# Chunk-selected attention with a top-1 expert layer: loads two pairs ahead, zero fill in four parts, sums folded earlier, bounds and row scalars in PSUM

## The chip, the cores and the metric

The kernel runs on one core of a Trainium2 chip. The metric is the device time of one launch in microseconds (us). Five engines work side by side, each taking its own instructions strictly in order: TensorE (PE, matmuls and transposes), VectorE (DVE), ScalarE (ACT), GpSimd (POOL) and SyncE (SP, which here only issues DMAs). They meet only through semaphores.

## The reference

Attention over 4 batches, 8 heads, 768 rows and 64 columns, in which each query keeps 6 of its causal chunks of 32 keys; then a top-1 mixture of experts with 8 experts, at most 80 tokens in each.

```python
ub = np.sum(np.maximum(q * k_min, q * k_max), axis=-1)     # bound of a chunk, 24 chunks
top_chunks = np.argsort(np.where(causal, ub, -1e9), axis=-1)[..., -6:]
scores = np.where(sel & (pos_q >= pos_k), q @ k.T / 8, -1e9)
attn = softmax(scores) @ v                                  # [4, 8, 768, 64]
x = attn.transpose(0, 2, 1, 3).reshape(3072, 512)
probs = softmax(x @ w_gate); e = argmax; keep the 80 highest gates of each expert
out[tok] = gate * (relu(x[tok] @ w1[e]) @ w2[e])            # all other rows are zero
```

## The kernel before, in words

Work goes by **pairs**: 16 pairs of heads (4 batches, 4 pairs each), one pair in one round of the main loop. For a pair the q, k and v of two heads lie side by side, 128 columns wide. In round i the program issues, in this order:

- `scores(i)`: six steps. In a step PE multiplies keys by queries into one of two PSUM tiles `SC` (L476), adds -65536 where a chunk was not selected (L482), and ACT takes the exponential into `EXB`, piece E0 to E5 (L487). POOL then zeroes the part above the diagonal in one block of the piece (the affine select, L492); for E0 the result goes to `ES` instead. POOL also adds the pieces into `ES`, column sums for the softmax, in the order of the table `ADDS` (L501).
- `bounds(i+1)`: PE forms the chunk bounds of the next pair (L442) in PSUM tiles `M0` and `MB`; DVE transposes them into `ubm`, adds the causal part, takes the eight largest of each row and marks in `uns` what was not selected (L446 to L457).
- `transposes(i+2)`: PE turns q and k of the pair after next (L418) in the two `SC` tiles; ACT and DVE copy them out, DVE takes minimum and maximum over chunks of 32 keys, and their difference (L426).
- `values(i)`: PE multiplies values by `EXB` (L512) in the two banks of `OB`, in the order of the table `AVS`. It reads each piece after its affine select, so the next-to-last piece of the first bank needs the select of E4 and the last of the second bank that of E5. ACT copies each bank to `oT` (L516).
- the load of v for pair i+2, then of q and k for pair i+3, all issued by SP; `unselT(i+1)`, PE's transpose of `uns` (L463); on POOL's own DMA queue one half of an expert's weights (L404, L407).
- `sums(i)`: PE multiplies `oT` by the gate weights (L522) and `ES` by ones (L527) into `M0`; DVE transposes that into `rows_s` and forms reciprocals (L530 to L532). Then `rows(i)`: PE turns `oT` back into rows in `OB` (L536), and DVE scales them (L544, L548); SP writes them to memory.
- after each fourth pair DVE works out the gates of the batch (L559 to L571), with one exponential on ACT (L563) that stands on ACT ahead of those of the next `scores`. DVE also takes rounds of a top-80 search, up to three in a pair from the fifth pair on (L597, L599).

After the loop come the last top-80 search, the slots, eight gathers, the expert matmuls and eight scatters. A helper, `op`, records for each buffer who wrote and read it last, and puts a semaphore wait ahead of an instruction that needs it; nothing else sets the order, so each engine's order is that of the program text. q and k have two buffers each: pair i+2 goes where pair i was. After round 1 the program also zeroes 2 KB in each partition of the last `w1s` and copies that over the whole 6 MB output in one DMA on SP (L654).

## Time and profile before

| | |
|---|---|
| median of three runs | 413.43 us (412.07 to 421.49) |
| the profiled execution | 414.83 us, span 412.6 us |
| mean granted TensorE clock | 0.896 of 2.4 GHz |
| busy: PE / DVE / POOL / ACT | 307.6 / 248.5 / 228.5 / 148.2 us |
| main loop, first exponential to last sum | about 20 to 333 us |
| moved by DMA | 47.49 MB, of it 28.32 MB on SP's queue and 18.67 MB on POOL's |

How to read it: a busy share over the whole span mixes the loop, which all engines share, with a tail of some 80 us that hangs on DVE and then on PE. What a change of the loop is worth is read from the loop: from the time between the same instruction of one pair and the next. POOL's affine select into `ES` is the first thing POOL does for a pair and comes once a pair, so its start times serve as the clock of the loop.

### The profile page before, as it was taken

To read this page: it belongs to the slowest core of one execution; us is meant where nothing else is said; L and a number is where in the kernel's file an instruction comes from. 1 tells how busy PE (TensorE), PEld (TensorE's weight loads), DVE (VectorE), ACT (ScalarE), POOL (GpSimd) and SP (SyncE) were. 2 spreads that over 40 slices of the span, in tenths; PEclk is the share of its full clock that TensorE was granted. 3 is DMA by queue.
4 is the path that set the end of the run, shared out by engine and by line. 5 is a ranking of instruction groups with operands and counts; after the bars stand their busy time and mean duration, and the time that the engine had idled before them with its cause. 6 is when DMAs were issued, how large, how long until landed. Compare 5 with 4: busy or idle time off the path is not lost.

```text
span 412.6 us, 7766 instructions
## 1 busy us (share of the span) xinstructions
PE 307.6 (75%) x3204; PEld 188.0 (46%) x3204; DVE 248.5 (60%) x604; ACT 148.2 (36%) x201; POOL 228.5 (55%) x297
## 2 busy tenths in 40 slices
PE   2598797918896999689989698896997730035994
PEld 2454555506463655456554455453553410014672
DVE  4554526132597769665987769596867259870332
ACT  2264353513536263427436253635253410001220
POOL 4085939390477475928595738568384960007132
PEclk9999898977999899899999899999898985555799
DMA  9807599999629495775749493939535170002012
GB/s 175 131 2 137 102 144 318 286 291 151 131 61 177 61 177 90 149 120 118 141 99 164 83 210 77 175 56 183 86 77 84 39 109 12 0 0 55 25 46 62
DMA packets 105011, 47.49 MB, mean 115 GB/s; under 512 B 89003, under 2 KB 97317, under 8 KB 104976
## 3 DMA queue, kind: packets, MB, share of 16 engines
q1 hardware_dynamic: 90896, 28.32, 30.8%
q0 software_dynamic: 13440, 18.67, 27.4%
q8 instruction: 25, 0.41, 0.4%
q10 hardware_dynamic: 640, 0.02, 0.1%
q14 instruction: 10, 0.08, 0.1%
HBM read 53.10 MB, written 10.75 MB: 155 GB/s over the span
## 4 chain that ended last, share of the span: by engine, by line
PE 40%; DMA 19%; issue 12%; POOL 10%; SPq 9%; DVE 5%; ACT 4%; POOLq 0%; DVEq 0%
PE OB L512 17%; DMA qn<-in_q_dram 11%; SPq L350 9%; DMA kn<-in_k_dram 8%; POOL ES L501 7%; PE SC L418 6%; PE SC L476 4%; PE OB L756 4%; PE SC L741 3%; ACT EXB L487 3%; PE M L527 2%; POOL EXB L492 1%; PE MB L463 1%; PE OB L536 1%; PE SC L482 1%
## 5 line engine op out<-in xcount | busy, mean ns | idle before, releaser
L501 POOL TENSOR_TENSOR ES<-ES,EXB 128x256 f32<-128x256 f32 (+1 forms) x112 | 107.5, 965 | 5.0
L487 ACT ACTIVATE EXB<-SC 128x1024 f32<-128x1024 f32 x96 | 85.9, 915 | 54.1 <-PE SC L482 52.5
L476 PE MATMUL SC<-qT,kT 64*128 64x512 f32 (+3 forms) x512 | 96.9, 466 | 6.4 <-ACT EXB L487 4.2
L512 PE MATMUL OB<-EXB,vn 128*64 128x256 f32 (+2 forms) x704 | 77.8, 378 | 0.0
L492 POOL TENSOR_SCALAR_AFFINE_SELECT ES<-EXB 128x256 f32<-128x256 f32 x16 | 6.4, 401 | 102.8 <-ACT EXB L487 102.8
L512 PEld LDWEIGHTS OB<-EXB,vn 128*64 128x64 f32 x704 | 49.1, 144 | 27.3 <-issue 13.3
L476 PEld LDWEIGHTS SC<-qT,kT 64*128 64x128 f32 x512 | 40.7, 186 | 44.5 <-ACT EXB L487 30.2
L501 POOL TENSOR_TENSOR ES<-EXB 128x768 f32<-128x768 f32 (+1 forms) x32 | 49.3, 1540 | 1.3
L516 ACT ACTIVATE oT<-OB 128x512 f32<-128x512 f32 (+1 forms) x32 | 15.7, 490 | 72.1 <-PE OB L512 72.1
L597 DVE MAX8 top<-cand 8x8 f32<-8x848 f32 (+1 forms) x40 | 40.3, 1008 | 1.9 <-ACT cand L578 1.3
L446 DVE STREAM_TRANSPOSE ubm<-M 128x160 f32<-128x160 f32 x16 | 5.6, 350 | 56.5 <-PE MB L442 56.5
L482 PE MATMUL SC<-unsT,ind 64*128 64x384 bf16 (+3 forms) x256 | 38.7, 296 | 0.0
L418 PE MATMUL SC<-ident_f,qn 128*128 128x128 f32 x96 | 15.6, 306 | 30.9 <-DMA qn<-in_q_dram 30.6
L492 POOL TENSOR_SCALAR_AFFINE_SELECT EXB<-EXB 128x256 f32<-128x256 f32 x80 | 31.5, 413 | 10.1 <-ACT EXB L487 10.1
L599 DVE MATCH_REPLACE8 cand<-top,cand 8x848 f32<-8x848 f32 (+1 forms) x36 | 35.7, 992 | 0.0
L422 DVE COPY kT<-SC 128x768 f32<-128x768 f32 x16 | 15.2, 952 | 25.2 <-PE SC L418 25.2
L418 PEld LDWEIGHTS SC<-ident_f,qn 128*128 128x128 f32 x96 | 11.8, 156 | 34.8 <-DMA qn<-in_q_dram 18.9
L420 ACT ACTIVATE qT<-SC 128x768 f32<-128x768 f32 x16 | 13.0, 810 | 35.2 <-PE SC L418 35.2
L530 DVE STREAM_TRANSPOSE rows_s<-M 128x192 f32<-128x192 f32 x16 | 6.0, 376 | 31.2 <-PE M L527 31.1
L418 PE MATMUL SC<-ident_f,kn 128*128 128x128 f32 x96 | 18.0, 339 | 7.3 <-DMA kn<-in_k_dram 5.5
L722 POOL DMA_INDIRECT qn<-x_rows,idx x4 | 3.9, 980 | 35.2 <-issue 35.2
L457 DVE TENSOR_TENSOR uns<-ubm,top 128x240 bf16<-128x240 f32 x16 | 20.3, 1272 | 0.5
(136 smaller groups left out, 432.1 us busy)
## 6 DMA issues: line engine op xcount, KB each, us to landing
w1s<-in_moe_w_dram POOLq DMA_DIRECT2D x8, 1024.0 KB, 10.7
w2s<-in_moe_w_dram POOLq DMA_DIRECT2D x7, 1024.0 KB, 10.6
qn<-in_q_dram SPq DMA_DIRECT2D x32, 192.0 KB, 6.8
...
```

What stands on the lines that cost most here:

```text
L350: op("sp", lambda: sp.dma_start(dst[s][:, :, h, :], a), w=[f"{nm}{s}{h}"], dsem=f"d_{nm}{s}{h}")
L418: op("pe", lambda: pe.transpose(SC[ps][:, ts(t)], a, ident_f[:]), r=[f"{nm}{s}0", f"{nm}{s}1", "ident_f"], w=[f"SC{ps}"], inc=(t == NT - 1))
L457: op("dve", lambda: ve.tensor_tensor(un, ubm[:, :, :, 0:NCH], thr, ALU.is_lt), r=["ubm"] + [f"top{t}{h}" for t in range(NT - 1) for h in r ...
L476: op("pe", lambda: pe.matmul(o, kT[j][pr, ts(kt)], qT[j][pr, q0:q1], start=True, stop=False), r=[f"kT{j}", f"qT{j}"], w=[f"SC{s}"], inc=False)
L482: op("pe", lambda: pe.matmul(o, ind[pr, ts(kt)], unsT[j][pr, b0 - 128:q1 - 128], start=False, stop=True), r=[f"ind{h}", f"unsT{j}"], w=[f" ...
L487: op("act", lambda: ac.activation(Ex(st, None, 0, W), src, ACTF.Exp, scale=SCALE), r=[f"SC{s}"], w=[f"E{st}"])
L492: op("gp", lambda: gp.affine_select(ad, a, pattern=[[0, 2], [1, 128]], compare_op=ALU.is_ge, fill=0.0, base=0, channel_multiplier=-1), r=[ ...
L501: op("gp", lambda: gp.tensor_tensor(o, in0, in1, ALU.add), r=[f"E{s2}", f"E{first[0]}"] if first else [f"E{s2}"] + kt, w=kt)
L512: op("pe", lambda: pe.matmul(OB[pr, q0:q1], vn[s][:, kt, h, :], ex, start=(n == 0), stop=last), r=[f"vn{s}{h}", "ES0" if st is None else f ...
L597: op("dve", lambda: ve.max(dst, cv), r=["cand"], w=[f"top{int(last)}{n}"])
L599: op("dve", lambda: ve.match_replace(cv, dst, cv, -2.0), r=["cand", f"top{int(last)}{n}"], w=["cand"])
L756: op("pe", lambda: pe.matmul(o, hTv(e)[:, fb * CAP:(fb + 1) * CAP], w2v(e)[:, fb, :], start=(fb == 0), stop=(fb == FB - 1)), r=[f"hT{s}{fb ...
```

## The change

Seven edits stand in the diff. (1) q and k of pair i+4 are loaded in round i right after `transposes(i+2)`, instead of pair i+3 after `values(i)`. (2) The zero fill is four DMAs of 1.5 MB, after rounds 2, 5, 8 and 11. (3) `ADDS` adds a piece in the step in which it was made, where before most adds stood behind the last step. (4) `rows(i)` stands ahead of `sums(i)`. (5) `ubm` and `rows_s` are views of `M0` in PSUM (columns 192 to 511), no longer in SBUF. (6) The difference of maximum and minimum is taken by POOL. (7) At the start: k of pair 0 goes over ACT's queue, ACT runs an exponential early, the gate weights come by two DMAs at the end of SP's first loads and two DVE copies, and `transposes(1)` stands ahead of `unselT(0)`.

```diff
     ADDS = [
-        [], [(1, 0, 128, 512)], [], [(2, 0, 256, 512)], [],
-        [(4, 0, 384, 512), (3, 256, 512, 768), (1, 384, 512, 640), (4, 384, 640, 768), (2, 256, 512, 768),
-         (4, 128, 512, 768), (5, 0, 640, 768)],
+        [], [(1, 0, 128, 512)], [(2, 0, 256, 512)], [(3, 0, 512, 768), (3, 256, 512, 768), (1, 384, 512, 640)],
+        [(4, 0, 384, 512), (4, 128, 512, 768), (4, 384, 640, 768)], [(5, 0, 640, 768)],
     ]
+
+    FIRST = {(1, 0): (0, 128), (3, 0): (2, 256)}
...
+                ubm = bass.AP(M0, 192, [[512, 128], [160, 2], [32, NT - 1], [1, 32]])
+                rows_s = bass.AP(M0, 192, [[512, 128], [32, NT], [1, 32]])
...
+                            op(eng, lambda: sy.queue[eng].dma_start(dst[s][:, :, h, :], a), w=[f"{nm}{s}{h}"], dsem=f"d_{nm}{s}{h}")
+
+                op("dve", lambda: ve.memset(dmy[:], 0.0), w=["dmy"])
+                load(0, "q")
+                load(0, "k", "acd")
+                load(1, "qk")
+                load(0, "v")
+                load(1, "v")
+                for h in range(2):
+                    src = bass.AP(moe_w_gate.tensor, moe_w_gate.offset + h * 64 * E, [[E, 64], [128 * E, NPB], [1, E]])
+                    op("sp", lambda: sp.dma_start(wgr[h * 64:(h + 1) * 64, :, :], src), w=[f"wgr{h}"], dsem=f"d_wg{h}")
+                op("act", lambda: ac.activation(dmy[:], dmy[:], ACTF.Exp), r=["dmy"], w=["dmy"])
...
-                load(1)
...
-                WG = [f"wg{p}{h}" for p in range(NPB) for h in range(2)]
+                for h in range(2):
+                    pr = slice(h * 64, h * 64 + 64)
+                    op("dve", lambda: ve.tensor_copy(wg[pr, :, h * E:(h + 1) * E], wgr[pr, :, :]), r=["wg", f"wgr{h}"], w=[f"wg{h}"])
+                WG = ["wg0", "wg1"]
...
-                    op("dve", lambda: ve.tensor_tensor(kmm[j][:, 1, 0:NCH], kmx[:], kmm[j][:, 0, 0:NCH], ALU.subtract),
+                    op("gp", lambda: gp.tensor_tensor(kmm[j][:, 1, 0:NCH], kmx[:], kmm[j][:, 0, 0:NCH], ALU.subtract),
...
-                        op("dve", lambda: ve.transpose(ubm[:, h, :, :].rearrange("p a b -> p (a b)"), ub[h][:, 0:160]),
+                        op("dve", lambda: ve.transpose(M0[:, 192 + h * 160:352 + h * 160], ub[h][:, 0:160]),
...
-                            op("dve", lambda: ve.max(top8[:, t, h, :], ubm[:, h, t, 0:4 * t + 8]), r=["ubm"], w=[f"top{t}{h}"],
-                               inc=(t == NT - 2 and h == 1))
+                            op("dve", lambda: ve.max(top8[:, t, h, :], M0[:, 192 + h * 160 + t * 32:196 + h * 160 + t * 36 + 4]),
+                               r=["ubm"], w=[f"top{t}{h}"], inc=(t == NT - 2 and h == 1))
...
-                    op("dve", lambda: ve.tensor_tensor(un, ubm[:, :, :, 0:NCH], thr, ALU.is_lt),
-                       r=["ubm"] + [f"top{t}{h}" for t in range(NT - 1) for h in range(2)], w=["uns"])
+                    uv = bass.AP(M0, 192, [[512, 128], [160, 2], [32, NT - 1], [1, NCH]])
+                    op("dve", lambda: ve.tensor_tensor(un, uv, thr, ALU.is_lt),
+                       r=["ubm", "M0"] + [f"top{t}{h}" for t in range(NT - 1) for h in range(2)], w=["uns"])
...
-                            first = {(1, 0): (0, 128), (3, 256): (3, 0)}.get((s2, c2))
+                            first = FIRST.get((s2, c2))
...
-                    op("dve", lambda: ve.transpose(rows_s[:].rearrange("p a b -> p (a b)"), M0[:, 0:192]), r=["M0"], w=["rows_s"])
-                    op("dve", lambda: ve.tensor_scalar(rden[:], rows_s[:, :, 16:18], 1e-9, None, ALU.add), r=["rows_s"], w=["rden"])
+                    op("dve", lambda: ve.transpose(M0[:, 192:384], M0[:, 0:192]), r=["M0"], w=["rows_s"])
+                    op("dve", lambda: ve.tensor_scalar(rden[:], rows_s[:, :, 16:18], 1e-9, None, ALU.add),
+                       r=["rows_s", "M0"], w=["rden"])
...
                 bounds(0)
+                transposes(1)
+                load(3, "qk")
                 unselT(0)
-                transposes(1)
                 for i in range(NP):
...
                         transposes(i + 2)
+                    if i + 4 < NP:
+                        load(i + 4, "qk")
                     rounds(i, 0, 1)
                     values(i)
                     if i + 2 < NP:
                         load(i + 2, "v")
-                    if i + 3 < NP:
-                        load(i + 3, "qk")
                     if i + 1 < NP:
                         unselT(i + 1)
                     rounds(i, 1, 2)
                     if i < NP - 1:
                         wload(i // 2, i % 2)
+                    rows(i)
                     sums(i)
-                    rows(i)
                     scale_rows(i)
                     if i % NPB == NPB - 1:
                         gate(i // NPB)
                         if i < NP - 1:
                             gate_digits(i // NPB)
                     rounds(i, 2, 3)
-                    if i == 1:
+                    if i % 3 == 2 and i < 12:
                         zk = f"w1_{E - 1}"
                         zr = bass.AP(w1s[E - 1], 0, [[DB * Fd, 128], [1, 2 * Dm]])
-                        op("dve", lambda: ve.memset(zr, 0.0), w=[zk])
-                        zs = bass.AP(w1s[E - 1], 0, [[DB * Fd, 128], [0, TOKT], [1, 2 * Dm]]).bitcast(F32)
-                        zd = bass.AP(out.tensor, out.offset, [[Dm, 128], [128 * Dm, TOKT], [1, Dm]])
-                        op("sp", lambda: sp.dma_start(zd, zs), r=[zk], w=["out"], dsem="d_zero")
+                        if i == 2:
+                            op("dve", lambda: ve.memset(zr, 0.0), w=[zk])
+                        g = i // 3
+                        zs = bass.AP(w1s[E - 1], 0, [[DB * Fd, 128], [0, NT], [1, 2 * Dm]]).bitcast(F32)
+                        zd = bass.AP(out.tensor, out.offset + g * NT * 128 * Dm, [[Dm, 128], [128 * Dm, NT], [1, Dm]])
+                        op("sp", lambda: sp.dma_start(zd, zs), r=[zk], w=[f"outz{g}"], dsem=f"d_zero{g}")
```

Three places as the instructions stand on the engines. First **POOL, one pair** (`ES` the sums, `EXB` the pieces E0 to E5; the last affine select, of 128x256, is that of E5). Before:

```order
L492 AFFINE_SELECT ES<-EXB 128x2x128
L492 AFFINE_SELECT EXB<-EXB 128x2x128
L501 TENSOR_TENSOR ES<-EXB 128x2x384
L492 AFFINE_SELECT EXB<-EXB 128x2x128 x2
L501 TENSOR_TENSOR ES<-ES,EXB 128x2x256
L492 AFFINE_SELECT EXB<-EXB 128x2x128
L492 AFFINE_SELECT EXB<-EXB 128x256
L501 TENSOR_TENSOR ES<-ES,EXB 128x2x128
L501 TENSOR_TENSOR ES<-EXB 128x2x256
L501 TENSOR_TENSOR ES<-ES,EXB 128x2x128 x2
L501 TENSOR_TENSOR ES<-ES,EXB 128x2x256 x2
L501 TENSOR_TENSOR ES<-ES,EXB 128x2x128
```

And in the changed kernel, from the select of E3 on:

```order
L502 AFFINE_SELECT EXB<-EXB 128x2x128
L511 TENSOR_TENSOR ES<-EXB 128x2x256
L511 TENSOR_TENSOR ES<-ES,EXB 128x2x256
L511 TENSOR_TENSOR ES<-ES,EXB 128x2x128
L502 AFFINE_SELECT EXB<-EXB 128x2x128
L511 TENSOR_TENSOR ES<-ES,EXB 128x2x128
L511 TENSOR_TENSOR ES<-ES,EXB 128x2x256
L511 TENSOR_TENSOR ES<-ES,EXB 128x2x128
L502 AFFINE_SELECT EXB<-EXB 128x256
L511 TENSOR_TENSOR ES<-ES,EXB 128x2x128
L435 TENSOR_TENSOR kmm<-kmx,kmm 128x24
```

The nine adds are of the same sizes, but the select of E4 has five of them ahead of it instead of two, and that of E5 eight instead of two.

Second **PE, the end of a pair**, with the semaphores that an instruction waits for (`sy_gp` is POOL's, `sy_act` ACT's): the last two pieces of `values`, `unselT`, then `rows` (L547) and `sums` (L532, L537) in the changed kernel.

```order
L522 MATMUL OB<-EXB,vn 64x128 [waits sy_gp]
L522 MATMUL OB<-EXB,vn 64x128
L473 MATMUL MB<-ident_bf,uns 128x128 [waits sy_dve]
L473 MATMUL MB<-ident_bf,uns 128x128 x4
L547 MATMUL OB<-ident_f,oT 128x128 [waits sy_act]
L547 MATMUL OB<-ident_f,oT 128x128 x5
L532 MATMUL M_22<-oT,wg 32x192 x4
L537 MATMUL M_22<-ES,onc 32x192 [waits sy_gp]
L537 MATMUL M_22<-ES,onc 32x192 x7
```

The six transposes of `rows` have moved ahead of the twelve matmuls of `sums`; the first row, the piece E5, waits for POOL as it did before.

Third **DVE, the first kT copy** (`wgr` receives the gate weights). Before:

```order
L396 CAST idc<-tmp_i 128x24
L398 CAST idc<-tmp_i 128x24
L422 COPY kT<-SC_20 128x768
L424 TENSOR_REDUCE kmm<-kT 128x24
L425 TENSOR_REDUCE kmx<-kT 128x24
```

And in the changed kernel:

```order
L402 CAST idc<-tmp_i 128x24 [waits sy_gp]
L404 CAST idc<-tmp_i 128x24 [waits sy_gp]
L407 COPY wg<-wgr 64x4x8 [waits sy_d_wg0]
L407 COPY wg<-wgr 64x4x8 [waits sy_d_wg1]
L431 COPY kT<-SC_20 128x768 [waits sy_pe]
```

Two copies that wait for the DMAs of the gate weights now stand in DVE's order ahead of the first kT copy.

## Rows read from the trace of the kernel before

**Rows 1.** Chain of work that ended last: shares of the span by line (page, part 4).

```profile
PE OB L512 17%; DMA qn<-in_q_dram 11%; SPq L350 9%; DMA kn<-in_k_dram 8%; POOL ES L501 7%; PE SC L418 6%; PE SC L476 4%; PE OB L756 4%; PE SC L741 3%; ACT EXB L487 3%; PE M L527 2%; POOL EXB L492 1%; PE MB L463 1%; PE OB L536 1%; PE SC L482 1%
```

**Rows 2.** Waits: engine line <- awaited: us in total, times, longest us.

```profile
PE SC L418 <- DMA qn<-in_q_dram: 30.6, 10, 10.2
PE M L527 <- POOL ES L501: 7.8, 6, 3.1
```

**Rows 3.** Timeline of POOL: start, length, engine, line, instruction, [idle before <- releaser].

```profile
21.78 0.41 POOL L492 TENSOR_SCALAR_AFFINE_SELECT ES<-EXB 128x256 f32<-128x256 f32 x1 [12.87 <-ACT EXB L487]
...
242.98 0.40 POOL L492 TENSOR_SCALAR_AFFINE_SELECT ES<-EXB 128x256 f32<-128x256 f32 x1 [7.82 <-ACT EXB L487]
...
255.94 0.91 POOL L407 DMA_DIRECT2D w2s<-in_moe_w_dram  x1
...
261.45 0.40 POOL L492 TENSOR_SCALAR_AFFINE_SELECT ES<-EXB 128x256 f32<-128x256 f32 x1 [4.59 <-ACT EXB L487]
...
318.71 0.40 POOL L492 TENSOR_SCALAR_AFFINE_SELECT ES<-EXB 128x256 f32<-128x256 f32 x1 [4.69 <-ACT EXB L487]
...
331.58 0.91 POOL L407 DMA_DIRECT2D EXB<-in_moe_w_dram  x1
```

**Rows 4.** Timelines of PE and ACT in pair 11.

```profile
240.52 1.13 PE L476 MATMUL SC<-qT,kT 64*128 64x512 f32 x4
...
249.46 0.44 PE L512 MATMUL OB<-ES,vn 128*64 128x128 f32 x4
...
254.15 0.45 PE L463 MATMUL MB<-ident_bf,uns 128*128 128x128 bf16 x5
254.29 0.38 ACT L516 ACTIVATE oT<-OB 128x256 f32<-128x256 f32 x1 [1.78 <-PE OB L512]
254.73 0.53 PE L522 MATMUL M<-oT,wg 128*32 128x192 f32 x8
256.05 0.86 PE L527 MATMUL M<-ES,onc 128*32 128x192 f32 x16 [0.79 <-POOL ES L501]
256.84 0.88 PE L536 MATMUL OB<-ident_f,oT 128*128 128x128 f32 x6
257.65 1.13 PE L476 MATMUL SC<-qT,kT 64*128 64x512 f32 x4
```

**Rows 5.** Groups by shape: line, instruction, count | busy us, mean ns | idle before.

```profile
L501 POOL TENSOR_TENSOR ES<-ES,EXB 128x512 f32<-128x512 f32 x48 | 61.0, 1271 | 2.5
L501 POOL TENSOR_TENSOR ES<-ES,EXB 128x256 f32<-128x256 f32 x64 | 46.5, 735 | 2.5
L457 DVE TENSOR_TENSOR uns<-ubm,top 128x240 bf16<-128x240 f32 x16 | 20.3, 1272 | 0.5
```

**Rows 6.** Timelines of SP's queue, DVE and PE at the start.

```profile
8.61 1.84 SPq L350 DMA_DIRECT2D vn<-in_v_dram  x2
9.04 0.95 DVE L422 COPY kT<-SC 128x768 f32<-128x768 f32 x1
12.11 0.47 PE L442 MATMUL M<-qT,kmm 64*32 64x160 f32 x1 [3.86 <-DVE kmm L426]
16.24 1.49 PE L418 MATMUL SC<-ident_f,qn 128*128 128x128 f32 x6
19.33 1.13 PE L476 MATMUL SC<-qT,kT 64*128 64x512 f32 x4 [0.32 <-ACT rq L421]
```

**Rows 7.** DMA of the gate weights (tile wg): landing.

```profile
DMA to landing us min/median/max: 3.4/4.1/4.3
```

**Rows 8.** Stretches: length, busy by engine, granted clock, DMA share, GB/s.

```profile
64.00:77.00 13.00, 10.91 (x99) 7.10 (x101) 7.34 (x21) 3.16 (x5) 8.09 (x10) 0.87 1.04 348
216.90:230.30 13.40, 10.03 (x118) 5.58 (x116) 10.07 (x26) 6.47 (x9) 8.31 (x13) 1.00 1.03 180
226.20:229.00 2.80, 0.13 (x8) 0.00 (x0) 2.47 (x14) 0.46 (x2) 2.80 (x5) 1.00 1.21 246
231.00:234.00 3.00, 2.97 (x14) 2.10 (x16) 1.39 (x2) 0.55 (x1) 2.81 (x3) 0.50 0.01 2
```

More of the change, by code (lines that the diff above doesn't have):

```diff
@@ L245, in _body @@
                 kmx = al(pers, "kmx", [128, NCH])
-                ubm = al(pers, "ubm", [128, 2, NT - 1, 32])
                 top8 = al(pers, "top8", [128, NT - 1, 2, 8])
@@ L270, in _body @@
                 wg = al(pers, "wg", [128, NPB, 32])
+                wgr = al(pers, "wgr", [128, NPB, E])
+                dmy = al(pers, "dmy", [128, 1])
                 onc = al(pers, "onc", [128, 2, 32])
-                rows_s = al(pers, "rows_s", [128, NT, 32])
                 rank_c = al(pers, "rank_c", [128, NT, E])
@@ L340, in iv, with load @@
                     return bass.AP(tmp_i, 0, [[160, rows]] + [list(d) for d in dims])
-                def load(i, what="qkv"):
+                def load(i, what="qkv", eng="sp"):
                     b, p, s = i // NPB, i % NPB, i % NB
@@ L349, in load @@
                             a = bass.AP(src.tensor, src.offset + base + h * S * D, [[D, 128], [128 * D, NT], [1, D]])
-                            op("sp", lambda: sp.dma_start(dst[s][:, :, h, :], a), w=[f"{nm}{s}{h}"], dsem=f"d_{nm}{s}{h}")
-                load(0)
+                            op(eng, lambda: sy.queue[eng].dma_start(dst[s][:, :, h, :], a), w=[f"{nm}{s}{h}"], dsem=f"d_{nm}{s}{h}")
[9 more added lines that the diff above has]
+                op("act", lambda: ac.activation(dmy[:], dmy[:], ACTF.Exp), r=["dmy"], w=["dmy"])
                 v128 = iv(128, [1, 128])
@@ L356, in _body @@
                 for j in range(2):
-                    op("dve", lambda: ve.memset(kmm[j][:], 0.0), w=[f"kmm{j}"])
+                    op("dve", lambda: ve.memset(kmm[j][:], 0.0), w=[f"kmm{j}", f"kmd{j}"])
                 op("dve", lambda: ve.memset(uns[:], 0.0), w=["uns"])
@@ L362, in _body @@
                     op("dve", lambda: ve.memset(onc[:, h, 16 + h:17 + h], 1.0), r=["onc"], w=[f"onc{h}"])
-                load(1)
-                for p in range(NPB):
-                    for h in range(2):
-                        src = bass.AP(moe_w_gate.tensor, moe_w_gate.offset + (p * 128 + h * 64) * E, [[E, 64], [1, E]])
-                        op("acd", lambda: ac.dma_start(wg[h * 64:(h + 1) * 64, p, h * E:(h + 1) * E], src),
-                           r=["wg"], w=[f"wg{p}{h}"], dsem="d_wg")
                 vc = iv(128, [1, 4])
@@ L544, in scale_rows @@
                     op("dve", lambda: ve.tensor_tensor(xo, xi, rx, ALU.mult), r=["O0", "O1", "rden"], w=["xp"])
-                    gi = bass.AP(rows_s, 0, [[NT * 32, 128], [32, NT], [E, 2], [1, E]])
+                    gi = bass.AP(M0, 192, [[512, 128], [32, NT], [E, 2], [1, E]])
                     go = bass.AP(lgp, 2 * p, [[NT * E * 2 * NPB, 128], [E * 2 * NPB, NT], [1, 2], [2 * NPB, E]])
                     rg = bass.AP(rden, 0, [[NT * 2, 128], [2, NT], [1, 2], [0, E]])
-                    op("dve", lambda: ve.tensor_tensor(go, gi, rg, ALU.mult), r=["rows_s", "rden"], w=[f"lgp{p}"])
+                    op("dve", lambda: ve.tensor_tensor(go, gi, rg, ALU.mult), r=["rows_s", "M0", "rden"], w=[f"lgp{p}"])
                     xdst = bass.AP(xd.tensor, xd.offset + b * S * Dm + p * 128, [[Dm, 128], [128 * Dm, NT], [1, 128]])
@@ L763, in down @@
                         out, bass.IndirectOffsetOnAxis(ap=idx[:, e:e + 1], axis=0), yv(e), None,
-                        bounds_check=NTOK - 1, oob_is_err=False), r=[yk(e), "idx", "out"], w=[f"out{e}"], dsem=f"d_o{e % 4}")
+                        bounds_check=NTOK - 1, oob_is_err=False), r=[yk(e), "idx"] + [f"outz{g}" for g in range(B)], w=[f"out{e}"], dsem=f"d_o{e % 4}")
                 for e in range(E):
```

2 lines of the change are left out of this document (1 added, 1 removed).

## Prediction

> **What bounds the kernel now.** I read the chain of waits first. In it stand PE's matmuls, but also the transfers of q and k and SP's issue of them, 28% of the span together [rows 1]: that is a chain through loads that come late, not an engine at its limit. The list of waits says where: PE's transposes stood 30.6 us for q, ten times [rows 2]. So I took POOL's first affine select of each pair as the clock of the loop: from the first pair at 21.78 to the last at 318.71 are 296.9 us for 15 steps [rows 3], 19.8 each.
>
> What would a step cost without late loads? Pair 11 has none, and its parts can be laid end to end. Scores start at 240.52 [rows 4], POOL's first select comes 2.46 later, at 242.98, and POOL works until it issues the weights at 255.94 [rows 3], 12.96 us of selects and adds. Then PE waits no longer: ones matmuls from 256.05 to 256.84, `rows` to 257.65, next scores [rows 4]. Sum: 2.46 + 12.96 + 0.11 + 0.79 + 0.81 = **17.13 us**, and POOL is the limit, since PE stood waiting for it before the ones matmuls (0.79 in this pair). After a fourth pair of a batch the step is 261.45 - 242.98 = 18.47 [rows 3], 1.34 more, because DVE and ACT work out the gates ahead of the next exponentials. Unhindered, the loop would be 12 x 17.13 + 3 x 18.47 = 261 us; 36 of the 297 are late loads and what follows them, a slower clock among it: after a stop of 2.8 us with PE all but empty the granted clock read 0.50 (1.2 GHz of 2.4) over the next transposes and values [rows 8].
>
> **The loads two pairs ahead.** Before, q and k for pair i+3 went out after `values(i)` and were wanted ahead of the next values, at most 12.4 us later (254.15 to 257.65, and 8.94 from scores to values) [rows 4]. Now they go out right behind `transposes(i+2)`, about 9 us into round i, and are wanted in round i+2: nearly two steps, over 30 us. The same DMAs, two of q and two of k, move past the two of v and past the rows' store on SP; v's wait, for the end of values, comes later than theirs, so nothing on SP is held up. A round's whole transfers, with half an expert's weights, kept the DMA engines active 13.4 us in their most crowded form [rows 8], less than a step. I take the late loads as gone: **-36 us**. The zero fill in parts adds no bytes: 6 MB near 350 GB/s is some 17 us [rows 8], 4 us per part, in front of transfers that have 30 us to land.
>
> **The adds as pieces come, and rows ahead of sums.** POOL does the same selects and adds, and in pair 11 it idled 0.7 us at most within them, so its 12.96 us stay. What moves is the selects: that of E5 now stands behind all adds but one. With 12.96 us of POOL's work and 0.74 for the last add [rows 5], plus a small gap, it ends 12.2 us after POOL's first select, 14.7 after the start of scores. Before, only two adds stood ahead of it. PE reads E5 in its last two value matmuls. Values begin 8.94 us after scores and end at 13.6 [rows 4], so PE, in order, now stands there until 14.7, after a first stop of about 0.6 at E4: three adds, two of 0.74 and one of 1.27 [rows 5], and a select of 0.4 stand between the two selects, so E4 is ready at 14.7 - 0.4 - 2.7 = 11.5, and PE comes to it at about 11.0. From the select of E5 to the next scores: 0.35 for the two matmuls (an estimate: the 48 of a pair take 4.7 us, and two can't overlap others), 0.5 from their end to `oT`, as from 254.2 to 254.73 [rows 4], `rows` 0.81, gate matmuls 0.35, ones matmuls 0.79, and 0.1 for semaphores. That is 14.7 + 2.9 = **17.55 us** a step. The sums no longer wait for POOL, whose last add ends before them; the wait has moved to the end of values, with `unselT`, `rows`, `sums` and the next scores queued behind it. The two edits, each sensible alone, together cost 0.42 x 12 = +5 us. At a batch's end `rows` lay beside DVE's reciprocals before and is now ahead of `sums`: the extra grows from 1.34 to about 2.1, the step to 19.6, +1.1 x 3 = +3.4. The last pair gets the same later sums, +1 us before the tail. Bounds: if PE did not stand at E5, the step would be POOL's own, 17.13 - 0.81 = 16.3; if the stop costs double, 18.
>
> **The start.** The gate weights' DMAs stand on SP behind ten loads, and two DVE copies that wait for them stand ahead of the first kT copy. Before, that copy ran at 9.04 and scores began at 19.33 [rows 6]. When do the weights land? In the trace they went over ACT's queue and landed 4.1 us after issue [rows 7]; SP had its twelve loads issued by 10.45 (8.61 + 1.84) [rows 6], so ten and two more are issued by about 9.5, and land at 13.5 by that row. If they queue behind every byte of 12 loads the row is the same or some later; at worst they share with the next four loads too and land at 17. I take 14, nearest the first row: kT at 14.2. The Trainium skill ("DMA: Bandwidth & Descriptors", Queues, rings and completion order) says that each engine consumes a queue's descriptors in ring order; it would put them behind all of SP's loads, nearer 14 than 13. No run here shows it, and the sum would differ by half a microsecond. From kT at 14.2: 3.07 as before, from 9.04 to 12.11 [rows 6], and 0.2 for POOL's difference, so bounds start at 17.5, 5.4 later. Of the 7.2 us from bounds to scores [rows 6] the two groups of transposes, 1.49 each, now lie beside DVE's work on the bounds; less 0.3 for ACT's copy behind them, 2.7 is saved. Net **+2.7 us** (+1.9 to +5.6 for landings at 13.5 to 17; -2.5 if the weights held nothing). Table load and k on ACT's queue lie in front of that wait and give nothing.
>
> **The rest.** PSUM views: DVE's select against the threshold averages 1272 ns for 240 elements [rows 5]; the kT copy reads PSUM at 0.95 us for 768 [rows 6], at which rate it would take 0.3, and ten maxima of 24 elements at most would lose no more than 0.3: -1.0 to +0.3 us a pair on DVE. That lies beside values (4.7 us): `uns` is wanted only by `unselT`. Uncovered, it would count in full. POOL's difference, at most an add of 0.74 [rows 5], lies with the weights' 0.91 [rows 3] in the 4.6 us between POOL's last add and its next select (17.55 - 12.96). Fewer of DVE's instructions now read two SBUF inputs, and here a rule bears on POOL. The rows: POOL's chain took 12.96 us in pair 11 with bounds on DVE and 12.87 in the last pair without any [rows 3], so DVE costs POOL 0.1 us a pair, 1.3 in all. The Trainium skill ("SBUF — State Buffer", Who interferes with whom) says that a DVE instruction with two SBUF inputs and a GpSimd one that reads SBUF exclude each other, whoever starts first. By it POOL might gain as long as such instructions last; by the rows DVE does nearly all the waiting, and I book nothing.
>
> **Sum.** 12 x 17.55 + 3 x 19.6 = 269.4 against 296.9: -27.5; start +2.7; tail +1: **-23.8 us**. The profiled execution took 414.83 (span 412.6) and would take 391.0; it lies 1.4 above the median of 413.43, against which the sum gives 389.6. I forecast **390 us**, chance 0.64; its own range, from steps of 17.2 to 17.9 and the bounds of the start, is 384 to 398.
>
> **Rivals.**
> *POOL alone sets the step*: PE reaches E5 later than I think, or the select comes earlier; then 16.3 a step and 18.4 at a batch's end. 12 x 16.3 + 3 x 18.4 = 250.8, 18.6 less than forecast: 371 us. For it: PE was never seen to stop long at a select. Against: the order of POOL's queue and its constant 12.9 us. 0.14.
> *The transfers were the limit, not their issue*: for it, 13.4 us of active DMA in a step of 17.55 is much, and with a 4 us zero part it is all of it. Against: 13.4 is for a round whose loads, weights and store fell together, and q and k now have two steps. If each part still delays one pair in full, 4 x 4 = 16 us: 406. 0.12.
> *The clock falls (slower)*: two new stops in each round, 0.6 and 0.7 us, beside the short ones on ACT, may leave PE's clock at 1.2 GHz from values on. For it: the fall after a stop of 2.8 us [rows 8]. Against: pair 11, with its 0.79 us stop, ran on unslowed. It decides if the stops come together to such a length, as in the last two pairs, which have no transposes. Price: at the lower clock six transposes took 1.49 instead of 0.88 [rows 6, 4]; `rows`, `sums` and first scores, 3 us on the path, would take some 5: 2 x 16 = 32 us, 422. The Trainium skill ("TensorE: Matmul & The Clock Gate", What's actually happening) says the gate falls back to 1.2 GHz when PE has been idle; the trace agrees, at 0.50. 0.04.
> The rest, 0.06, is for loads that stay late for a reason I do not see, 400 to 413.
>
> The **range** takes in the forecast's own and most of the second rival: 378 to 402 us, leaving out the first and third. A measurement of this kernel tells 2%, some 8 us, from no change: below 405 us is faster. Faster 0.88 (forecast, first rival, most of the second), the same 0.08, slower 0.04.
>
> **What would show it.** In the new profile: no PE wait for q or k of more than a microsecond after the first; about 17.5 us from select to select; PE's waits for POOL at the value matmuls, over 10 us in sum, and hardly any at the ones matmuls; the first kT copy near 14 us; the clock at 1.00 through the loop. I am wrong if steps are 16.3 with no such stop, if transposes still wait for DMA, or if kT is copied at 9.

## The result

The changed kernel takes **392.83 us** (median of four runs, 391.83 to 393.25) against 413.89 us for the kernel before in runs beside it (412.07 to 421.49). The ratio is 0.952, with a 95% interval from 0.947 to 0.957: faster. On another chip the pair stood at 397.63 to 418.55 us, ratio 0.959 (0.949 to 0.969). The forecast was 390 us, range 378 to 402.

The profiled execution took 393.25 us, span 391.5, mean granted clock 0.913. Here is its chain of waits, which answers to [rows 1].

```profile
POOL ES L511 33%; PE SC L486 8%; POOL EXB L502 7%; PE OB L522 5%; ACT EXB L497 5%; PE OB L770 4%; PE OB L547 4%; PE SC L755 3%; PE M L537 3%; SPq L353 2%; PE M L532 2%; PE SC L492 2%; ACT oT L526 2%; PE SC L427 1%; DMA wgr<-in_moe_w_gate_dram 1%
```

The transfers of q and k, with SP's issue 28% of the span before, are gone but for 2% of issue. POOL's adds and selects (L511, L502) now hold 40%: the loop hangs on POOL's order. The list of waits (us in total, times, longest us) says at which instructions; it answers to [rows 2].

```profile
PE OB L522 <- POOL EXB L502: 22.1, 28, 3.1
...
PE SC L427 <- DMA qn<-in_q_dram: 6.2, 1, 6.2
DVE wg L407 <- DMA wgr<-in_moe_w_gate_dram: 5.0, 1, 5.0
```

PE waits for q once, at the very start, where it was ten times and 30.6 us. The wait for POOL ahead of the ones matmuls (7.8 before) is off the list. In its place PE stands 28 times, nearly twice in each pair, ahead of a value matmul, until POOL has done the affine select of E4 or E5; 5.5 of the 22.1 us are two stops in the last two pairs, which have no transposes. One pair shows both stops: POOL first, then PE and ACT (start, length, engine, line, instruction, [idle before <- releaser]). It answers to [rows 3, 4].

```profile
208.51 0.40 POOL L502 TENSOR_SCALAR_AFFINE_SELECT ES<-EXB 128x256 f32<-128x256 f32 x1 [3.52 <-ACT EXB L497]
...
211.83 0.41 POOL L502 TENSOR_SCALAR_AFFINE_SELECT EXB<-EXB 128x256 f32<-128x256 f32 x1
212.32 1.28 POOL L511 TENSOR_TENSOR ES<-ES,EXB 128x512 f32<-128x512 f32 x1
213.55 0.41 POOL L502 TENSOR_SCALAR_AFFINE_SELECT EXB<-EXB 128x256 f32<-128x256 f32 x1
214.04 1.27 POOL L511 TENSOR_TENSOR ES<-EXB 128x512 f32<-128x512 f32 x1
215.40 2.08 POOL L511 TENSOR_TENSOR ES<-ES,EXB 128x512 f32<-128x512 f32 x2
217.43 0.41 POOL L502 TENSOR_SCALAR_AFFINE_SELECT EXB<-EXB 128x256 f32<-128x256 f32 x1
217.92 2.76 POOL L511 TENSOR_TENSOR ES<-ES,EXB 128x256 f32<-128x256 f32 x3
220.64 0.41 POOL L502 TENSOR_SCALAR_AFFINE_SELECT EXB<-EXB 128x256 f32<-128x256 f32 x1
221.13 0.72 POOL L511 TENSOR_TENSOR ES<-ES,EXB 128x256 f32<-128x256 f32 x1
221.81 0.24 POOL L435 TENSOR_TENSOR kmm<-kmx,kmm 128x24 f32<-128x24 f32 x1
...
226.42 0.40 POOL L502 TENSOR_SCALAR_AFFINE_SELECT ES<-EXB 128x256 f32<-128x256 f32 x1 [3.66 <-ACT EXB L497]
```

```profile
206.06 1.13 PE L486 MATMUL SC<-qT,kT 64*128 64x512 f32 x4
...
217.89 2.60 PE L522 MATMUL OB<-EXB,vn 128*64 128x128 f32 x28 [0.74 <-POOL EXB L502]
221.10 0.44 PE L522 MATMUL OB<-EXB,vn 128*64 128x128 f32 x4 [0.60 <-POOL EXB L502]
221.47 0.45 PE L473 MATMUL MB<-ident_bf,uns 128*128 128x128 bf16 x5
221.61 0.38 ACT L526 ACTIVATE oT<-OB 128x256 f32<-128x256 f32 x1 [2.61 <-PE OB L522]
222.05 0.87 PE L547 MATMUL OB<-ident_f,oT 128*128 128x128 f32 x6
222.85 0.53 PE L532 MATMUL M<-oT,wg 128*32 128x192 f32 x8
223.20 0.83 PE L537 MATMUL M<-ES,onc 128*32 128x192 f32 x16
223.96 1.13 PE L486 MATMUL SC<-qT,kT 64*128 64x512 f32 x4
```

Read the step along the path that sets it. Scores start at 206.06 and POOL's first select comes 2.45 later. From there POOL works without a pause but 0.66 us before its second select, as before, until E5's select ends, 220.64 + 0.41 = 221.05: 12.54. PE then takes E5's values (221.10), `rows`, gates and ones, and starts the next scores at 223.96: 2.91. Sum **17.90**, and 226.42 - 208.51 = 17.91 is the step.

The start, from the timelines of SP's queue and DVE, answers to [rows 6]:

```profile
10.25 1.51 SPq L363 DMA_DIRECT2D wgr<-in_moe_w_gate_dram  x2
...
14.17 0.44 DVE L407 COPY wg<-wgr 64x32 f32<-64x32 f32 x2 [5.04 <-DMA wgr<-in_moe_w_gate_dram]
14.64 0.96 DVE L431 COPY kT<-SC 128x768 f32<-128x768 f32 x1
```

DVE stands 5.04 us for the gate weights, and the first kT copy comes at 14.64 instead of 9.04. The first and last pair's select:

```profile
25.18 0.41 POOL L502 TENSOR_SCALAR_AFFINE_SELECT ES<-EXB 128x256 f32<-128x256 f32 x1
...
300.73 0.40 POOL L502 TENSOR_SCALAR_AFFINE_SELECT ES<-EXB 128x256 f32<-128x256 f32 x1 [4.46 <-ACT EXB L497]
```

So the loop is 275.55 us for 15 steps, 296.93 before. A stretch of four pairs (length, busy by engine in the order PE, PEld, DVE, ACT, POOL, then granted clock, DMA share, GB/s) shows that the clock held, which answers to [rows 8]:

```profile
25.00:98.00 73.00, 64.70 (x702) 37.67 (x700) 28.96 (x95) 33.68 (x46) 52.26 (x69) 1.00 0.73 146
```

### The profile page after: what moved, and what is told of

It is laid out like the page before. It is cut to its first block, busy times and chain, and to the rows that moved or that the text cites. A ratio compares the mean times of both kernels' runs of the same rounds, so it can differ in the third digit from the quotient of the medians.

```text
span 391.5 us, 7778 instructions
## 1 busy us (share of the span) xinstructions
PE 299.9 (77%) x3204; PEld 181.5 (46%) x3204; DVE 222.6 (57%) x591; ACT 148.5 (38%) x202; POOL 233.0 (60%) x313
## 4 chain that ended last, share of the span: by engine, by line
POOL 41%; PE 31%; issue 12%; ACT 6%; DVE 3%; SPq 3%; DMA 1%; POOLq 0%
POOL ES L511 33%; PE SC L486 8%; POOL EXB L502 7%; PE OB L522 5%; ACT EXB L497 5%; PE OB L770 4%; PE OB L547 4%; PE SC L755 3%; PE M L537 3%; SPq L353 2%; PE M L532 2%; PE SC L492 2%; ACT oT L526 2%; PE SC L427 1%; DMA wgr<-in_moe_w_gate_dram 1%
## 5 line engine op out<-in xcount | busy, mean ns | idle before, releaser
L511 POOL TENSOR_TENSOR ES<-ES,EXB 128x256 f32<-128x256 f32 (+1 forms) x112 | 106.9, 961 | 7.8
L486 PE MATMUL SC<-qT,kT 64*128 64x512 f32 (+3 forms) x512 | 98.6, 473 | 8.2 <-ACT EXB L497 6.5
L522 PE MATMUL OB<-EXB,vn 128*64 128x256 f32 (+2 forms) x704 | 81.0, 374 | 22.1 <-POOL EXB L502 22.1
L522 PEld LDWEIGHTS OB<-EXB,vn 128*64 128x64 f32 x704 | 45.9, 141 | 54.9 <-POOL EXB L502 35.0
L486 PEld LDWEIGHTS SC<-qT,kT 64*128 64x128 f32 x512 | 41.7, 190 | 48.3 <-ACT EXB L497 32.2
L511 POOL TENSOR_TENSOR ES<-EXB 128x768 f32<-128x768 f32 (+1 forms) x32 | 49.3, 1541 | 2.7
L502 POOL TENSOR_SCALAR_AFFINE_SELECT ES<-EXB 128x256 f32<-128x256 f32 x16 | 6.4, 401 | 61.1 <-ACT EXB L497 60.9
L455 DVE STREAM_TRANSPOSE M<-M 128x160 f32<-128x160 f32 x16 | 5.8, 365 | 61.9 <-PE MB L451 61.9
L502 POOL TENSOR_SCALAR_AFFINE_SELECT EXB<-EXB 128x256 f32<-128x256 f32 x80 | 33.1, 413 | 10.1 <-ACT EXB L497 10.1
L540 DVE STREAM_TRANSPOSE M<-M 128x192 f32<-128x192 f32 x16 | 6.3, 397 | 57.3 <-PE M L537 57.3
L492 PEld LDWEIGHTS SC<-unsT,ind 64*128 64x128 bf16 x256 | 13.1, 96 | 14.5 <-issue 11.3
L776 POOL DMA_INDIRECT out_dram<-EXB,idx x8 | 7.4, 921 | 15.9 <-DVE EXB L774 12.9
L747 ACT ACTIVATE rq<-MB 128x320 bf16<-128x320 bf16 x4 | 1.7, 437 | 39.4 <-PE MB L744 39.4
```

Source lines behind the costliest of these rows:

```text
L486: op("pe", lambda: pe.matmul(o, kT[j][pr, ts(kt)], qT[j][pr, q0:q1], start=True, stop=False), r=[f"kT{j}", f"qT{j}"], w=[f"SC{s}"], inc=False)
L492: op("pe", lambda: pe.matmul(o, ind[pr, ts(kt)], unsT[j][pr, b0 - 128:q1 - 128], start=False, stop=True), r=[f"ind{h}", f"unsT{j}"], w=[f" ...
L502: op("gp", lambda: gp.affine_select(ad, a, pattern=[[0, 2], [1, 128]], compare_op=ALU.is_ge, fill=0.0, base=0, channel_multiplier=-1), r=[ ...
L511: op("gp", lambda: gp.tensor_tensor(o, in0, in1, ALU.add), r=[f"E{s2}", f"E{first[0]}"] if first else [f"E{s2}"] + kt, w=kt)
L522: op("pe", lambda: pe.matmul(OB[pr, q0:q1], vn[s][:, kt, h, :], ex, start=(n == 0), stop=last), r=[f"vn{s}{h}", "ES0" if st is None else f ...
```

## The experiments

All of them cut the span at the same four marks: the first pair's select (start), the last pair's select (loop, 15 steps), the first eight-maximum of the last top-80 search (last pair), the end. The runs from `loads_only` to `wg_late` shared a chip, those from `sums_first` to `sbuf_kmd` another, and the last four rows a third; "again" is a second profile of a kernel. An ordinary step is any but the three at a batch's end and the last.

| kernel | start | loop | last pair | behind | span | ordinary step |
|---|---|---|---|---|---|---|
| before | 21.78 | 296.93 | 21.12 | 72.77 | 412.6 | 17.1 to 21.5 |
| changed | 25.18 | 275.55 | 23.09 | 67.68 | 391.5 | 17.90 |
| `loads_only` | 21.83 | 262.15 | 24.41 | 66.81 | 375.2 | 17.14 |
| `adds_back` | 25.02 | 254.92 | 21.47 | 66.89 | 368.3 | 16.29 |
| `half_fold` | 24.93 | 264.74 | 22.82 | 67.61 | 380.1 | 17.08 |
| `wg_late` | 18.86 | 275.86 | 23.93 | 66.95 | 385.6 | 17.89 |
| `sums_first` | 24.78 | 261.85 | 21.98 | 71.49 | 380.1 | 17.08 |
| `both` | 19.39 | 251.27 | 21.36 | 71.48 | 363.5 | 16.28 |
| `sbuf_kmd` | 19.57 | 252.25 | 21.07 | 71.81 | 364.7 | 16.35 |
| before, again | 21.77 | 295.78 | 24.39 | 71.56 | 413.5 | 17.1 to 22.2 |
| changed, again | 24.60 | 275.51 | 22.52 | 71.97 | 394.6 | 17.92 |
| `zero_one` | 24.81 | 275.77 | 22.34 | 72.48 | 395.4 | 17.89 |
| `both`, again | 19.75 | 254.86 | 21.63 | 71.76 | 368.0 | 16.30 |

### The early loads alone

The kernel before with edit (1) and nothing else: q and k of pair i+4 behind `transposes(i+2)`, and one load of pair 3 ahead of the loop; the zero fill is still one DMA.

```diff
+                load(3, "qk")
...
+                    if i + 4 < NP:
+                        load(i + 4, "qk")
                     rounds(i, 0, 1)
...
-                    if i + 3 < NP:
-                        load(i + 3, "qk")
```

> The kernel before with one edit alone: q and k of pair i+4 loaded right behind the transposes of pair i+2, zero fill still one DMA of 6 MB. My theory, late loads cost 36 us: no wait of PE for q or k over 1 us in the loop, steps of 17.1 and 18.5, 378 us (375 to 382). Rival, that the 6 MB in front of the loads are too much for two pairs' lead: a stop of 5 to 10 us remains near the fifth pair, 383 to 388.

Measured: 377.77 us (377.39 to 381.43), ratio 0.921 (0.913 to 0.929). Its waits:

```profile
PE M L527 <- POOL ES L501: 15.6, 16, 3.1
...
PE SC L418 <- DMA qn<-in_q_dram: 4.8, 1, 4.8
```

The loop of 262.15 is the 261 us that the prediction had worked out from a single undisturbed pair. One edit of the seven gives more than all of them: the other six together cost some 15 us.

### The adds put back

The changed kernel with the table `ADDS` (and `FIRST`) of before; `rows` stays ahead of `sums`.

```diff
-        [], [(1, 0, 128, 512)], [(2, 0, 256, 512)], [(3, 0, 512, 768), (3, 256, 512, 768), (1, 384, 512, 640)],
-        [(4, 0, 384, 512), (4, 128, 512, 768), (4, 384, 640, 768)], [(5, 0, 640, 768)],
+        [], [(1, 0, 128, 512)], [], [(2, 0, 256, 512)], [],
+        [(4, 0, 384, 512), (3, 256, 512, 768), (1, 384, 512, 640), (4, 384, 640, 768), (2, 256, 512, 768),
+         (4, 128, 512, 768), (5, 0, 640, 768)],
```

> The changed kernel with the table of adds of before (all adds but two behind the selects of E4 and E5), all else as changed. My theory, that the selects of E4 and E5 come late because the adds stand ahead of them on POOL: PE's waits for POOL at the value matmuls (22.1 us in the changed kernel) fall under 2 us, POOL's own work sets the step, 16.4 us instead of 17.9 and 18.5 instead of 20.0 at a batch's end, 369 us (367 to 373). Rival, that POOL's 12 us of work sets the step in any order: 392 us, with PE's wait moved back to the ones matmuls.

Measured: 369.98 us (369.44 to 370.07), ratio 0.899 (0.892 to 0.905). In its timelines of POOL and PE in one pair

```profile
144.87 0.76 POOL L503 TENSOR_SCALAR_AFFINE_SELECT EXB<-EXB 128x256 f32<-128x256 f32 x2
145.61 1.27 POOL L512 TENSOR_TENSOR ES<-ES,EXB 128x512 f32<-128x512 f32 x1
146.83 0.77 POOL L503 TENSOR_SCALAR_AFFINE_SELECT EXB<-EXB 128x256 f32<-128x256 f32 x2
147.56 0.73 POOL L512 TENSOR_TENSOR ES<-ES,EXB 128x256 f32<-128x256 f32 x1
...
149.61 4.93 POOL L512 TENSOR_TENSOR ES<-ES,EXB 128x256 f32<-128x256 f32 x5
```

```profile
148.30 4.49 PE L523 MATMUL OB<-EXB,vn 128*64 128x384 f32 x44
...
153.30 0.88 PE L548 MATMUL OB<-ident_f,oT 128*128 128x128 f32 x6
...
154.59 0.86 PE L538 MATMUL M<-ES,onc 128*32 128x192 f32 x16
```

all selects have ended at 147.6, before PE's value matmuls on `EXB` begin at 148.30; 44 value matmuls run in one piece; and the adds end at 154.5, just when PE comes to the ones matmuls, since `rows` has taken up the 0.8 us in which it used to wait. The same six selects and nine adds in another order are worth 1.61 us in each ordinary step, 20.6 us in the loop and 22.8 us between the medians.

### Half of the fold

Only E4's three adds are moved back behind E5's select; those of E2 and E3 stay where the change has them.

```diff
-        [(4, 0, 384, 512), (4, 128, 512, 768), (4, 384, 640, 768)], [(5, 0, 640, 768)],
+        [], [(4, 0, 384, 512), (4, 128, 512, 768), (4, 384, 640, 768), (5, 0, 640, 768)],
```

> The changed kernel with the three adds of E4 moved behind the select of E5: five adds ahead of E5's select instead of eight, E4's as before with five. My theory: PE still stops about 0.75 us at E4 in each pair and no longer at E5, steps of 17.1 instead of 17.9, 380 us (378 to 384). If only the total of POOL's work counts: 392 us. If the stop at E4 alone made the loss: 392 us too, but with PE's wait for POOL at the value matmuls as large as now.

Measured: 382.12 us (380.91 to 382.53), ratio 0.928 (0.921 to 0.935). PE's wait for the selects falls from 22.1 us at 28 places to 14.1 at 15, and the step to 17.08. Each stop goes with the adds ahead of its own select, as it should if the order of POOL's queue is the cause: with three adds fewer ahead of E5's select its stop of 0.60 is gone, and that at E4, where nothing was changed, stays at 0.71 to 0.79 us in most pairs.

### The sums ahead of the rows

`adds_back` with edit (4) undone as well.

```diff
-                    rows(i)
                     sums(i)
+                    rows(i)
```

> The run adds_back (table of adds of before in the changed kernel) with sums ahead of rows, as before. My theory: POOL's last add then has the rows' transposes behind it on the path, 0.81 us, so steps are 17.1 instead of 16.3 and 18.4 unchanged at a batch's end, 12 x 0.82 = 10 us: 379.5 us (378 to 381). If the order of rows and sums is of no weight: 370.

Measured: 381.88 us (381.77 to 382.83), ratio 0.922 (0.916 to 0.928). That is 0.9 above the range: the loop is only 6.9 us longer than that of `adds_back`, since three ordinary steps of `adds_back` were longer than 16.3 (16.64 twice, 18.27); the part behind the loop, 4.6 us longer on this chip, makes up the rest. The wait ahead of the ones matmuls is back, in each pair:

```profile
PE M L538 <- POOL ES L512: 14.8, 16, 3.1
```

With the adds last, `rows` first is worth 17.08 - 16.29 = 0.79 us a step. With the fold it should be worth nothing, since there POOL's last add ends at 221.85 and PE comes to the ones matmuls at 223.20, after 0.81 us of `rows`. That is argued from the rows; the fold without `rows` first was not run.

### The gate weights' copies moved

The two DVE copies of edit (7) stand just ahead of the main loop.

```diff
-                for h in range(2):
-                    pr = slice(h * 64, h * 64 + 64)
-                    op("dve", lambda: ve.tensor_copy(wg[pr, :, h * E:(h + 1) * E], wgr[pr, :, :]), r=["wg", f"wgr{h}"], w=[f"wg{h}"])
...
                 unselT(0)
+                for h in range(2):
+                    pr = slice(h * 64, h * 64 + 64)
+                    op("dve", lambda: ve.tensor_copy(wg[pr, :, h * E:(h + 1) * E], wgr[pr, :, :]), r=["wg", f"wgr{h}"], w=[f"wg{h}"])
                 for i in range(NP):
```

> The changed kernel with the two DVE copies of the gate weights moved from ahead of the first kT copy to just ahead of the main loop. My theory, that the first pair stood for these weights: kT copy near 9.2 instead of 14.64, POOL's first select near 20 instead of 25.18, 387.5 us (386.5 to 389). Rival, that the loads of pair 1 hold the start anyway, since q of pair 1 lands after 10 us and its transposes stand ahead of the first scores: select at 23, 391 us.

Measured: 386.78 us (386.0 to 387.95), ratio 0.940 (0.934 to 0.945). The first kT copy is back at 9.04 and the start is 18.86, 2.92 before that of the kernel before: the rest of the new start does gain, as the prediction's bound of -2.5 for weights that held nothing had it, and two 0.18 us copies in DVE's order took 6.3 us.

### Both mended

`adds_back` and `wg_late` in one kernel.

> The changed kernel with the table of adds of before and with the copies of the gate weights just ahead of the main loop. The two gave 22.9 and 6.1 us alone, at different places (steps of the loop, and the start), so my theory is that they add: 364 us (363 to 365.5), steps of 16.3 and 18.4, first select near 19. Rival, that a loop that starts 6 us earlier meets loads that are still landing: some of the 6 us comes back as waits of the first transposes, 366 to 370.

Measured: 366.35 us (364.94 to 368.09), ratio 0.885 (0.877 to 0.892). It ran again on the further chip, beside the changed kernel:

> Adds put back behind the selects and the gate weights' copies moved behind the start, beside the changed kernel on one chip. From steps of 16.28, 16.63 and 18.39 against 17.9 and 20.0 and a start of 19.4 against 25.2 I expect it 28 us shorter (26 to 30) where both have the same part behind the loop: 364 to 366 us if that of the changed kernel is 67.7 here, and both longer by 5 if it is 72.

Measured there: 367.59 us (365.16 to 369.77), ratio 0.884 (0.872 to 0.895), 30.0 less than the changed kernel's 397.63, at the edge of what was expected, and below the 369 to 371 us that a part behind the loop of 72 us would have given. With the next kernel it is the fastest of the study. The first result lies 2.4 above its forecast; the part behind the loop, 71.48 instead of the 67 that the forecast took over, more than accounts for it, as the loop came out 3.7 us shorter than that of `adds_back`. That difference is the clock: in `adds_back` and in the second profile of `both` one step takes 18.27 and the last 17.83 and 17.72, with a granted clock between 0.50 and 0.66 in part of them, where the first profile of `both` has 16.64 and 16.25 at 1.00.

### Bounds and row scalars in SBUF, the difference on DVE

`both` with edits (5) and (6) undone.

```diff
+                ubm = al(pers, "ubm", [128, 2, NT - 1, 32])
+                rows_s = al(pers, "rows_s", [128, NT, 32])
...
-                    op("gp", lambda: gp.tensor_tensor(kmm[j][:, 1, 0:NCH], kmx[:], kmm[j][:, 0, 0:NCH], ALU.subtract),
+                    op("dve", lambda: ve.tensor_tensor(kmm[j][:, 1, 0:NCH], kmx[:], kmm[j][:, 0, 0:NCH], ALU.subtract),
```

> As the run both, but with the bounds and row scalars in SBUF and the difference of maximum and minimum on DVE, as before. My theory: DVE's select against the threshold goes back from 0.41 to over 1.2 us and the difference to over 0.5, some 2 us a pair, and all of it lies beside the value matmuls: 364 us, within 1.5 of the run both. Rival, that with steps of 16.3 DVE is near its limit in pairs with three search rounds (some 14.5 us of work): rows and sums come late to DVE and the next bounds stand, 0.5 to 1 us in nine pairs, 369 to 373.

Measured: 366.41 us (365.61 to 374.09), ratio 0.883 (0.877 to 0.889), the same as `both`. By groups of one shape (count | busy us, mean ns of one | idle before), first `both`, then this kernel; they answer to [rows 5]:

```profile
L509 POOL TENSOR_TENSOR ES<-ES,EXB 128x512 f32<-128x512 f32 x48 | 61.1, 1273 | 2.5
...
L465 DVE TENSOR_TENSOR uns<-M,top 128x240 bf16<-128x240 f32 x16 | 6.5, 407 | 0.6
...
L557 DVE TENSOR_TENSOR lgp<-M,rden 128x96 f32<-128x96 f32 x16 | 5.2, 322 | 0.0
```

```profile
L509 POOL TENSOR_TENSOR ES<-ES,EXB 128x512 f32<-128x512 f32 x48 | 61.1, 1273 | 2.5
...
L433 DVE TENSOR_TENSOR kmm<-kmx,kmm 128x24 f32<-128x24 f32 x16 | 18.1, 1133 | 0.5
L557 DVE TENSOR_TENSOR lgp<-rows_s,rden 128x96 f32<-128x96 f32 x16 | 16.9, 1054 | 0.0
...
L465 DVE TENSOR_TENSOR uns<-ubm,top 128x240 bf16<-128x240 f32 x16 | 12.2, 760 | 0.5
```

The three DVE instructions with two SBUF inputs take 2.2 us more of DVE in a pair than with one input in PSUM (or on POOL). POOL's adds take 1273 ns in both. The select against the threshold came back to 0.76 us only, not to over 1.2; single ones take 0.41 to 1.55 us. The gain is real on DVE and lies beside the path that sets the step.

### The old loads

The changed kernel with edit (1) undone.

```diff
-                load(3, "qk")
...
-                    if i + 4 < NP:
-                        load(i + 4, "qk")
...
                         load(i + 2, "v")
+                    if i + 3 < NP:
+                        load(i + 3, "qk")
```

> The changed kernel with q and k of pair i+3 loaded after values(i), as before; zero fill in four parts, all else as changed. My theory: the late loads cost what they cost before, 36 us less what a longer step hides: PE's waits for q and k over 20 us in sum, 420 to 432 us, slower than the kernel before although everything else of the change is in it. Rival, that the zero fill in parts had removed the worst of the waits (a 10 us stop in the fourth pair): 400 to 410.

Measured: 417.13 us (412.77 to 422.15), ratio 1.004 (0.998 to 1.010). That is just under the range expected, and well above the rival's. The waits of its profiled execution (span 420.4) have the old entry again:

```profile
PE SC L427 <- DMA qn<-in_q_dram: 24.8, 10, 6.3
```

Without the early loads the rest of the change makes the kernel no faster, as far as this measurement can tell. What the fold costs with them hides here in part, as the stops at the selects fall to 9.2 us at 8 places: a step that waits for q comes later to everything.

### The zero fill in one DMA, and the part behind the loop

The changed kernel with edit (2) undone; and, on the same chip, the changed kernel and the one before once more.

```diff
-                    if i % 3 == 2 and i < 12:
+                    if i == 2:
...
```

> The changed kernel with the zero fill in one DMA again, all else as changed. With the loads two pairs ahead I expect the one fill of some 17 us to delay one round by at most 1 us, as the one step of 19.47 against 18.5 in the kernel with the early loads alone: steps 17.9 and 20.0, time within 1.5 us of the changed kernel. The rival is that the four parts are what hides the fill: then PE waits for q about 10 us in one round as in the kernel before, and the time is 8 to 12 us more.

> The changed kernel once more, for its part behind the loop: from the first MAX8 of the search over all experts to the end it took 67.7 us in its first profile, 72.8 in the kernel before. If that difference of 5 us belongs to the chip or the execution, the kernel before, profiled on this chip, has the same length here as this one within 1 us; if it belongs to the change, the kernel before is 5 longer again. Time 392 to 395 us.

> The kernel before, profiled on the same chip as the changed one. Theory that the 5 us behind the loop belong to the chip or the execution: from the first MAX8 of the search to the end within 1 us of the changed kernel's. Rival, that they belong to the change: 72 to 73 here against 67 to 68 there.

Measured: `zero_one` 397.87 us (396.42 to 398.79), the changed kernel 397.63 (396.3 to 398.87): the same, with steps of 17.89 and 20.0 and no second wait for q. With loads two pairs ahead the four parts do nothing; that the fill cost the kernel before its longest wait for q of 10.2 us [rows 2] was not tried by itself.

The changed kernel came out 3 us above what was expected of it. The part behind the loop tells why: 71.97, and 71.56 in the kernel before. The 5 us by which the first pair of profiles differed there are not from the change. They arise on PE at the up-projection of the second of the eight experts and behind it, as in the timeline of the changed kernel on this chip:

```profile
360.45 1.38 PE L755 MATMUL SC<-rq,w1s 128*128 128x80 bf16 x15
362.31 0.28 PE L755 MATMUL SC<-rq,w1s 128*128 128x80 bf16 x3 [0.49 <-issue]
363.02 0.20 PE L755 MATMUL SC<-rq,w1s 128*128 128x80 bf16 x1 [0.43 <-issue]
363.74 0.31 PE L755 MATMUL SC<-rq,w1s 128*128 128x80 bf16 x4 [0.52 <-issue]
...
365.45 3.58 PE L770 MATMUL OB<-w2s,qT 128*80 128x512 bf16 x8
```

In its first profile both experts' matmuls ran without a gap:

```profile
359.21 2.33 PE L755 MATMUL SC<-rq,w1s 128*128 128x80 bf16 x32
...
361.61 2.34 PE L755 MATMUL SC<-rq,w1s 128*128 128x80 bf16 x32
363.74 2.26 PE L770 MATMUL OB<-w2s,qT 128*80 128x512 bf16 x8
```

From the second expert's first matmul to the start of the down-projection (L770) pass 5.00 us instead of 2.13. The gaps that the profile shows are 2.4 us of that. The down-projection then takes 1.3 us more, at a granted clock of 0.50 (366 to 368) instead of 0.88 (364 to 366). Together these make 4.2 of the 4.3 us by which the two profiles of the changed kernel differ behind the loop. What PE's sequencer waits for in these gaps no row shows, and it stays open: the DMA view has one transfer of instructions (0.02 MB) around them in the long profile, and the same in the short one.

## Why the prediction was right, and where its terms were off

- **Late loads, -36.** Right. The loop of `loads_only` is 34.8 us shorter than before (262.15 against 296.93), and `old_loads` takes back the whole gain. The rival that the transfers themselves are the limit falls with it: that loop moves the same bytes.
- **The selects behind the adds.** Right in kind: both stops are where the text put them, 0.74 and 0.60 us against 0.6 and 0.7, the wait at the ones matmuls is gone, and what follows E5's select takes 2.91 of the 2.9 foretold. The term that was mis-sized is POOL's chain. I said that POOL's 12.96 us stay and that E5's select ends 12.2 after the first; it ends 12.54 after it, and the step is 17.90, not 17.55. The rows show where: before, E2 and E3's selects stood in a row, and so did E4's and E5's, 0.77 for two (0.76 and 0.77 in the rows of `adds_back`, with the next add 0.74 and 0.73 behind their start). Now each of the four stands alone and the next instruction starts 0.49 behind its start, as 217.43 to 217.92: 1.96 in place of 1.47. Of these 0.49 us 0.15 come back among the adds, and the whole chain to the end of the last add takes 221.81 - 208.51 = 13.30 against 12.96 [rows 3]. At eleven ordinary steps of 17.9 that is 4 us, at three batch ends (20.0 against 19.6) 1.2, and the last step of 18.49 adds 0.9: 275.55 instead of 269.4. Of this 0.9 some 0.6 is a slower clock (see the other rivals).
- **The start, +2.7.** It is +3.40, and +2.83 in the second pair of profiles. The weights landed 3.3 to 3.9 us after their issue, as the row of before had it; but SP came to them at 10.25, not by 9.5, so kT ran at 14.64. On the rule of the Trainium skill ("DMA: Bandwidth & Descriptors", Queues, rings and completion order) that I had cited: the last load of v, issued at 9.19, landed 4.7 us later, at 13.9, the weights at 14.1 and 14.4; that agrees with ring order but would read the same without it.
- **The last pair, +1.** +1.97 in the first profiles, -1.87 in the second: the kernel before alone spreads from 21.12 to 24.39 there. Not told apart.
- **The rest, nothing.** Right for the PSUM views and POOL's difference: `sbuf_kmd` equals `both`. On the exclusion of a GpSimd and a two-input DVE instruction that the Trainium skill ("SBUF — State Buffer", Who interferes with whom) states as symmetric: DVE's side of it is plain here (407 against 760 ns, 322 against 1054); POOL's does not show (1273 ns in either kernel), as the rows of before had it.
- **Behind the loop, nothing foretold.** -5.1 in the first profiles, +0.4 in the second. So the 390 came nearer than its own terms: start, loop and last pair gave -16.0 against -23.8 forecast (+3.4, -21.4, +2.0), and a stretch behind the loop that the changed kernel shows at either length (67.68 and 71.97) made up 5.1 of the missing 7.8. That much of the nearness is luck.
- **The other rivals.** POOL alone setting the step, 16.3 and 18.4 at a batch's end, 371 us, is what `adds_back` does (16.29, 18.40, 369.98), so the steps of that case were priced right and only its condition was not met; its loop is 254.92, not 250.8, and a part behind the loop of 66.89 hides that in the sum. The clock as a whole did not fall: 1.00 over these four pairs in spite of both stops, and 0.96 to 1.00 in each quarter of the loop. It fell in two short stretches: behind the second batch's end (granted 0.50 in part of 173 to 177 us, in a step of 18.05), and, where that rival had looked, in the last pairs. In the last of the 15 steps PE stops 2.4 us for E4's select in either profile of the changed kernel. The stretch behind the stop, first profile, then second (columns as in the stretch of four pairs, the clock third from the end):

```profile
292.00:296.00 4.00, 4.00 (x33) 2.41 (x29) 1.63 (x3) 0.68 (x2) 3.84 (x6) 0.60 0.00 0
292.00:296.00 4.00, 3.28 (x37) 2.05 (x32) 1.60 (x3) 1.30 (x3) 3.84 (x6) 1.00 0.00 0
```

With 0.60 the last step is 18.49 us, with 1.00 it is 17.90, like the others: after the same stop the clock fell in one execution and not in the other.
